# Six attention units load q in plain rows, under another instruction table, in a fused attention and bilinear-FFN kernel

## The chip, the core and the metric

The kernel runs on one core of a Trainium2 chip. A core has a matrix engine (TensorE, PE in the profile; its weight loads are PEld), a vector engine (VectorE, DVE), an activation engine (ScalarE, ACT), a general engine (GpSimd, POOL) and SyncE (SP), which here only issues DMAs. Each engine takes its instructions in program order and waits on semaphores for data of the others. The metric is the device time of one execution in microseconds (us); the time of a kernel is the median of its runs.

## The reference

```python
# attention, inside each chunk of 64 tokens: q, k, v are (8, 8, 576, 64)
scores = (1 / sqrt(64)) * q_c @ k_c^T      # 64x64 for each batch, head, chunk
attn   = softmax(scores)
out    = attn @ v_c
# FFN: x is (4608, 512); w_a, w_b (512, 1536); w_out (1536, 512)
x = out.transpose(0, 2, 1, 3).reshape(4608, 512)
y = ((x @ w_a) * (x @ w_b)) @ w_out
```

Inputs and output are float32; the kernel computes in bfloat16 with float32 sums.

## The kernel before

The 4608 tokens are nine blocks (K = 0 to 8) of 512 tokens; a block is two units of 256 tokens (units 0 to 17), and a unit is four chunks of 64 tokens with all eight heads. Blocks 0 to 3 and 5 to 8 lie in one batch entry each; block 4 (units 8 and 9) collects the ninth chunk of all eight.

**A unit of attention.** q, k and v of a unit come from HBM by DMA (`load_paired`, `load_natural`, `load_split`, all through `load`, L359) into float32 buffers `f`, of which there are two sets (even and odd units). A cast to bfloat16 (`cast_natural` for q and k into `qkb`, `cast_v` for v into `vb`, both through the helper at L330) goes to ACT, DVE or POOL as the table says. One DMA transposes q and k together (`turn_dma`, L684) into `qkT`. The scores are 32 matmuls of 64x64 (L732) into two banks; two ACT instructions take the exponential of a bank each, 128x512, and write it to `E` in bfloat16 (`part_scores`, L884). From unit 8 (`FROM`) on the values are 32 matmuls with `E` as weights and `vb` as the moving operand (L792, `part_first` and `part_second`, 16 each); DVE takes the reciprocals of the sums and multiplies (L806, L808), and a DMA transposes the block (`turn_x`, L690) into `xT`. Units 4 to 7 use another form with separate sums and values (L742, L770).

**Paired rows.** For units in `PAIRED` (4 to 17) q is loaded with two tokens side by side in a partition, so that the DMA moves runs of 512 bytes: one DMA of 512 KB for a unit within one batch entry (`load_paired`). For other units q is loaded as k is, in rows of 256 bytes, by two DMAs of 256 KB (`load_natural`). The cast of a paired q writes with a rearranged pattern, and the query order inside a chunk is then (r, q) in place of token order. For units of `PAIRED` from 8 on the exponential puts this right: it writes `E` through `p (a q r) -> p a r q`, so that consecutive elements go to every second bfloat16. Units below 8 put it right in a later DVE multiplication.

**The FFN.** Blocks 1 to 8 use a scheme with seven products in place of eight for each of the two input products (L1008, four matmuls of 128x128 by 256 columns each) and for the output product (L1313, six matmuls; L1151 for block 8). ACT and DVE copy and add the results between products (L330, L1046, L1341), and DVE or POOL make sums of inputs and of weights (L968, L1270, L1042). Block 0 uses plain products (L919).

**The order.** Everything that the kernel does is a list of operations numbered as they are made. The text `ORDER_OF_ALL` is a table of words: a letter for the engine (a: PE, b: ACT, c: DVE, d: POOL, e: SP or ACT issuing a DMA), the operation's number, and for PE the PSUM banks that it takes (of eight). Each engine runs its words in the table's order. The words were made beforehand by a planner with a cost for each operation; `c_act(n)` is the cost of an ACT instruction of n columns, 0.591 us for 512. When the kernel is built the costs are no longer used: only the table and the operations' data dependences count. A POOL operation also waits for the last bfloat16 operation of DVE ahead of it in the table.

Of the kernel before, what the change touches and what calls it, by code (L numbers as in the profile page):

```python
# [97 lines left out]
c211 d266 a344 e275 c342 b347 a349:7 b345 e44 a339:3 c215 d278 a353 e276 c340 a359:1 a350 a348:0 d268 d272 c219 b354  # L98
c355 b351 b360 c352 a372:3 c373 d356 a357:5 b358 c371 a361 c362 a365 c366 a367 c368 b47 a375 e38 a363 b376 a379:3 a377
c364 d41 d253 d45 b378 a390:4 a381 b382 c343 c383 a380:6 a384 a388:0 a401:7 b279 c249 c255 a403:2 a396 e223 b385 a394  # L100
a392 b389 a406 d242 c386 a398 b39 b391 d228 d254 c397 b407 c402 a408 c404 b393 a412 b413 a431:3 e225 b229 c399 c244
a432 a411:7 a419:2 c241 c250 c243 c252 b409 a415 b416 a420 b421 c270 e280 a317:56 a422 b319 b423 b318 e230 a434 e277
# [3 lines left out]
c418 a447:0 a534:5 a449:7 a527:4 e301 b325 c430 e304 e324 b326 e327 b448 a544 a530 b531 a525:1 d461 c450 a532 b533  # L106
c456 a536 a567:2 d469 a539 e323 e500 c526 d462 a535:6 a555:1 c528 c537 a546 a569:4 d464 d446 b306 e473 b540 c538 c541
e504 c568 b307 b547 a548 c549 b570 a556 e474 c470 c542 d471 d465 a590 a550 c551 a552 c553 e308 d335 a594:0 a592 a585:7
c586 a587:5 c588 b591 a596 a603:6 b593 b545 b597 c598 a595:7 a599 d466 e506 b600 e503 a607 b604 b608 c557 c601 a611
c612 a620:5 a609 c610 a613 c614 d529 c621 a625 b626 d472 d602 a496:12 b498 a336:04 b338 c615 a558 a559 a605:7 b337  # L110
a488:25 e475 c560 e476 b497 a514:40 b489 e459 e305 a631 a622:1 c606 c623 e477 c632 a627 c628 b516 d589 d467 b515 b517
a563 a564 b490 b491 a518:20 c520 c519 d485 d316 a492:41 a629:5 a646 c493 c633 a634 a630:0 a561:2 e499 e502 e505 d624
d554 d638 a562 e501 c494 a644:4 b565 b635 c636 a648 c468 c639 c641 b511 b647 c649 e507 a708:1 a650 c651 e460 d616 e659
a642:6 a652 c653 b645 a715 a710:7 b643 a713 a750:5 d640 c716 a722 c709 a718:0 a752:1 c654 e478 b512 a571 c714 a719
c566 e457 c711 a572 a717:7 c723 d637 c724 a574 a735 e481 e479 e510 e509 e480 b486 b720 a729 c721 b753 a733 a775 e508
a731 d581 c736 c751 b730 b776 c734 c573 a773 e513 b774 a770:0 c771 a768:6 c769 c732 a779 a680:73 a575 c576 a782 c783
a777:0 a778:6 c784 d618 d521 b681 b780 b682 a693:74 c697 c695 c698 d655 d617 d656 d737 e487 a522:23 b524 a790 a792
e484 e482 e483 d666 d657 b495 b523 b791 e685 c725 c781 c696 e458 e688 a796 c797 d619 d582 a726:3 d583 c793 a727 a794
c795 a694:47 d712 d584 d772 d658 b728 a669:25 c673 a670:61 c677 c678 c699 a741 a788:0 e686 c674 c701 c675 c700 a742
a786:1 c702 a813:5 b789 e689 e580 e579 e684 c671 c672 c676 a810 c811 a805:4 b787 a808 c809 a803:7 a744:2 e683 b690  # L120
a814 a817 c804 c806 c818 e661 e665 c819 b691 a738:6 a739 c740 a745 e703 c815 a812:7 a835 b743 a746 a747 b748 c816 a829
b830 a831 a827:4 c807 c766 c836 c749 b828 a825:6 b826 e660 e687 b667 d821 c822 c824 c764 a833 c832 c834 a754 a842:5
e692 a755 b756 a847 b848 b704 a844:1 a849 b850 c843 a757 d798 d823 a853 c837 a920:0 b854 a758 a882:73 d765 d785 c845
a851:5 c759 c855 e668 d801 d820 d840 d799 e662 e664 e578 e663 a856 b857 a852:1 a863 c858 b884 a918:2 c919 e896 e874
e900 a867 c868 b921 b864 e902 e899 a865 c866 b883 a951:3 c952 a956 a953:6 c954 a869 b957 a962 b963 c870 a958 b959
a932:57 a705:43 a933:61 b707 e577 b706 c935 c941 c936 d800 d679 c937 c942 c938 a973 b974 a965 b966 a860:5 c939 a906:31
c838 d839 d871 a907:47 c912 c914 c908 c913 c940 e873 e875 e872 e877 a961:2 c967 c915 a861 b903 b862 a960:4 a971:6 c972
c910 c911 c964 a975 a888 a889 a969:7 d841 a977 e897 c909 a979 a993 c890 e878 e945 c978 c980 c994 a986:1 a988:3 b970
d846 e762 c981 a885:4 a886 c987 d955 a991 b992 e901 e898 b880 a891:2 a892 a1000 e763 e876 c989 b1001 a997 c802 c887
d859 a893 a995:1 c976 b998 c999 a894 a1012 b1013 d879 d767 b895 e881 c947 c948 a1016 c1017 d1004 a996:3 a1027:4  # L130
a1008:0 b1009 a1010:7 a922 a923 a1025:1 d1005 c1002 c949 a1018 b904 c1007 c1006 b1011 c924 c1028 a1030 c1026 a1014
b1031 c1019 c917 e905 a1035:5 a1032 b1033 d968 d916 c1015 c990 e1081 e1079 d1020 a1036 e1058 b1037 a1034:4 c1038
a1103:1 e761 e1056 a1039 b1040 d1003 d1021 d982 a925 a1101:3 c1041 a926 c927 e760 b946 e1082 e931 a1050 c1051 a1138:6
b1104 b1102 c1139 a1046 a1048 b1047 c1049 a1052 a934:24 a1065:60 b1066 b1067 a1140:7 c1053 c1023 c1141 e1055 a1145
a1143 a1119:56 a1120:07 c1126 e1080 b944 d1042 c1127 d1142 c1124 c1128 c1125 d1022 c1129 c1122 c1123 d1054 d1024
a1043:4 b1146 a1152 b1144 a1149 b943 a1089:06 a1090:27 c1095 c1097 c1091 c1096 c1098 b1153 a1044 a1147:5 b1150 c1151
a1148:2 c1154 a1156:7 a1162 d1155 c1093 c1092 b1157 b1045 a1164 c1165 a1178 c983 c1094 a1068:0 a1166 c1167 c1029 e1057
d1087 a1173:5 c1174 b1179 a1184 b1185 c985 a1158:6 c1159 c984 c1168 a1160 a1071 b1062 e1132 d1191 d1192 b1161 c1163
a1074:2 a1075 a1199 a1175:5 c1176 d1169 e1060 e1084 b1086 b1063 a1180 a1072 b1073 a1069 a1182:3 c1070 a1183:1 b1181
c1186 a1187 b1188 a1076 a1195:5 b1196 b1200 c1189 e930 e1083 c1194 d1193 d1177 e1085 b1133 a1203 c1204 a1197:0 a1217  # L140
c1218 c1198 d950 d1190 a1205 c1206 a1222:7 a1212:3 c1213 d1134 a1201 a1077 b1078 a1219 a1214:1 c1215 c1100 a1223 c1202
b1220 b1224 a1105 a1106 a1233 b1107 a1226 b1227 a1221:3 a1108 c1135 c1170 c1225 e1061 e1059 d1099 e1267 e1088 a1252:16
b1254 c1228 a1109 c1110 a1237 a1288:4 a1235 c1238 b1234 c1236 a1239 b1289 b1253 a1326 c1240 b1327 a1302:65 c1307
a1303:23 c1311 c1309 c1305 d1136 d1207 e1064 a1121:10 e1270 e1269 c1310 e1242 e1111 e1247 e1268 c1306 a1321:7 e1113
a1332 c1322 c1308 c1312 a1290:2 c1291 a1255:6 b1130 b1131 d1210 a1276:10 a1277:75 c1284 c1280 a1323:3 c1282 c1281
c1324 c1278 b1333 a1343 b1344 a1328 a1330:0 c1334 c1279 e1272 c1283 d1216 a1339:4 a1331:3 c1340 d1208 d1229 d1209
d1137 d1211 d1172 c1285 b1329 a1335 b1274 e1117 e1248 b1336 c1337 a1347 c1348 c1325 e928 a1230:1 a1361 a1231 a1341:7
c1342 a1356:5 c1357 a1349 c1350 a1358:0 c1359 b1362 a1363 a1367 a1365:5 a1345 b1364 a1261:3 a1262 b1368 a1382 b1383
a1370 d1241 e929 e1245 e1266 e1315 a1378:0 a1366:4 c1232 e1116 a1258 d1338 d1351 c1369 b1379 c1374 c1360 c1375 a1400
a1259 c1346 c1352 d1171 d1377 b1273 b1371 c1372 a1386 c1387 b1260 b1401 a1384 c1385 c1373 c1376 a1380:2 a1388 c1389  # L150
c1381 a1404:5 a1395:7 a1263 a1256 a1406 c1396 b1407 e1246 e1243 a1397:4 b1286 e1244 e1118 e1271 e1115 c1257 e1275
d1317 d1250 c1318 a1264 b1265 a1402 b1403 c1408 b1249 c1398 a1450:7 c1287 a1420 c1421 a1416 c1417 d1390 a1479:6 d1391
d1353 c1393 c1392 a1409 a1292 a1293 b1451 b1410 a1425:45 c1480 d1316 d1354 a1405:0 c1411 a1418 c1419 e1114 e1251 c1412
a1295 a1296 c1297 a1422 c1423 d1399 a1452:6 a1484 b1427 b1426 d1355 a1464:54 c1468 b1294 a1465:12 a1304:30 c1466 c1470
b1453 a1486 b1485 a1490 e1298 b1314 a1481:0 d1424 d1394 c1469 c1472 c1471 c1467 c1473 d1319 b1313 a1440:41 a1439:35
# [20 lines left out]
def kernel(  # L176
# [159 lines left out]
    def c_act(n):  # L336
        return 0.156 + n * 0.00085
# [1360 lines left out]
```

## Time and profile before

| | |
|---|---|
| median of 3 runs | 291.56 us (291.33 to 291.64) |
| the profiled execution, its own time | 291.75 us |
| its span, first to last instruction | 290.0 us |
| ACT busy | 171.5 us (59%) x292 |
| DVE busy | 244.8 us (84%) x484 |
| POOL busy | 181.5 us (63%) x176 |
| DMA packets | 133304, 57.71 MB, mean 199 GB/s |

The span leaves out 1.75 us of the execution's own time. A busy time counts any moment at which the engine has an instruction in work, so a matrix engine that is busy nearly all the time may still lose time in short waits: these are seen in the distance between the starts of its groups of matmuls.

### The profile page before, as it was taken

To read this page: it belongs to the slowest core of one execution; us is meant where nothing else is said; L and a number is where in the kernel's file an instruction comes from. 1 tells how busy PE (TensorE), PEld (TensorE's weight loads), DVE (VectorE), ACT (ScalarE), POOL (GpSimd) and SP (SyncE) were. 2 spreads that over 40 slices of the span, in tenths; PEclk is the share of its full clock that TensorE was granted. 3 is DMA by queue.
4 is the path that set the end of the run, shared out by engine and by line. 5 is a ranking of instruction groups with operands and counts; after the bars stand their busy time and mean duration, and the time that the engine had idled before them with its cause. 6 is when DMAs were issued, how large, how long until landed. Compare 5 with 4: busy or idle time off the path is not lost.

```text
span 290.0 us, 8654 instructions
## 1 busy us (share of the span) xinstructions
PE 284.4 (98%) x3508; PEld 233.5 (81%) x3508; DVE 244.8 (84%) x484; ACT 171.5 (59%) x292; POOL 181.5 (63%) x176
## 2 busy tenths in 40 slices
PE   7999999999999999999999999999999999999995
PEld 3555458888887888888888888888888888888884
DVE  2777989999988999996897889679979787988972
ACT  3875897879658746636826674846456743245111
POOL 4626268737689688919758685689838954653130
PEclk9999999999999999999999999999999999999999
DMA  7999999879999898876997893998881540021025
GB/s 248 390 397 402 291 304 328 221 171 243 229 181 234 242 215 242 196 151 163 259 247 190 213 288 85 222 205 240 193 200 41 178 111 0 2 110 38 0 107 186
DMA packets 133304, 57.71 MB, mean 199 GB/s; under 512 B 103952, under 2 KB 124560, under 8 KB 133264
## 3 DMA queue, kind: packets, MB, share of 16 engines
q1 hardware_dynamic: 132032, 56.05, 72.0%
q10 hardware_dynamic: 1232, 1.11, 1.1%
q8 instruction: 27, 0.44, 0.6%
q14 instruction: 13, 0.11, 0.1%
HBM read 37.75 MB, written 9.44 MB: 163 GB/s over the span
## 4 chain that ended last, share of the span: by engine, by line
PE 91%; DVE 4%; DMA 1%; ACT 1%; issue 1%; POOL 0%; DVEq 0%; ACTq 0%
PE F L1008 49%; PE F L1313 23%; PE F L919 7%; PE F L1151 3%; PE F L528 2%; PE F L732 1%; PE F L1642 1%; PE F L792 1%; DMA f<-in_k_dram 1%; ACT E L884 1%; DVE wst L1255 1%; DVE bsb L1046 1%; DVE AB L1046 1%; DVE AB L1042 0%; DVE osb L1341 0%
## 5 line engine op out<-in xcount | busy, mean ns | idle before, releaser
L330 ACT COPY part<-F 128x512 f32<-128x512 f32 x94 | 54.2, 590 | 57.1 <-PE F L1008 37.4
L1042 POOL TENSOR_TENSOR AB<-AB,bsb 128x512 bf16<-128x512 bf16 x43 | 49.5, 1157 | 27.7 <-DVE AB L1042 9.4
L1046 DVE TENSOR_TENSOR bsb<-F,part 128x512 bf16<-128x512 f32 x72 | 49.0, 684 | 6.3 <-PE F L1008 4.8
L1270 POOL TENSOR_TENSOR wst<-AB 128x512 bf16<-128x512 bf16 x31 | 35.6, 1155 | 12.9 <-DVE wst L968 4.3
L1008 PEld LDWEIGHTS <-WA 128*128 128x128 bf16 x384 | 37.2, 98 | 5.1 <-issue 0.3
L1008 PEld LDWEIGHTS <-WB 128*128 128x128 bf16 x384 | 37.2, 98 | 4.7 <-issue 0.3
L330 ACT COPY wst<-F 128x512 f32<-128x512 f32 (+1 forms) x42 | 23.4, 570 | 29.4 <-PE F L1313 12.2
L1046 DVE TENSOR_TENSOR AB<-F,part 128x512 bf16<-128x512 f32 x48 | 32.9, 685 | 6.5 <-PE F L1008 3.1
L1313 PEld LDWEIGHTS <-AB 128*128 128x128 bf16 x288 | 28.0, 98 | 3.5 <-issue 0.2
L1008 PEld LDWEIGHTS <-Ta 128*128 128x128 bf16 x288 | 28.0, 98 | 3.4
L1008 PEld LDWEIGHTS <-Tb 128*128 128x128 bf16 x288 | 27.7, 98 | 3.7 <-issue 0.2
L1313 PEld LDWEIGHTS <-wst 128*128 128x128 bf16 x288 | 28.0, 98 | 3.3
L1008 PE MATMUL F<-wst,WB 128*128 128x256 bf16 x192 | 28.8, 273 | 0.1
L1008 PE MATMUL F<-wst,Ta 128*128 128x256 bf16 x192 | 28.8, 273 | 0.0
L1008 PE MATMUL F<-wst,Tb 128*128 128x256 bf16 x192 | 28.8, 273 | 0.0
L1008 PE MATMUL F<-xT,WA 128*128 128x256 bf16 x192 | 28.7, 273 | 0.0
L1008 PE MATMUL F<-wst,WA 128*128 128x256 bf16 x192 | 28.7, 273 | 0.0
L1008 PE MATMUL F<-xT,WB 128*128 128x256 bf16 x192 | 28.3, 273 | 0.0
L330 ACT CAST qkb<-f 128x1024 bf16<-128x1024 f32 (+1 forms) x25 | 24.3, 983 | 3.7 <-DMA f<-in_k_dram 3.7
L1313 PE MATMUL F<-WO,AB 128*128 128x256 bf16 x192 | 25.2, 273 | 0.2 <-ACT E L884 0.2
L884 ACT ACTIVATE E<-F 128x512 bf16<-128x512 f32 x32 | 21.1, 699 | 5.3 <-PE F L732 5.2
L1270 POOL TENSOR_TENSOR spare_sum<-AB,wst 128x512 bf16<-128x512 bf16 x17 | 19.6, 1154 | 6.7 <-DVE WB L956 3.5
(137 smaller groups left out, 542.4 us busy)
## 6 DMA issues: line engine op xcount, KB each, us to landing
f<-in_k_dram SPq DMA_DIRECT2D x28, 256.0 KB, 4.8
out_dram<-osb SPq DMA_DIRECT2D x28, 256.0 KB, 2.9
f<-in_q_dram SPq DMA_DIRECT2D x12, 512.0 KB, 5.6
f<-in_v_dram SPq DMA_DIRECT2D x40, 128.0 KB, 3.5
f<-in_v_dram SPq DMA_DIRECT2D x16, 256.0 KB, 5.3
wst<-in_moe_w_b_dram SPq DMA_DIRECT2D x6, 512.0 KB, 8.6
wst<-in_moe_w_a_dram SPq DMA_DIRECT2D x6, 512.0 KB, 8.9
wst<-in_moe_w_out_dram SPq DMA_DIRECT2D x6, 512.0 KB, 4.4
```

The source lines that it names most:

```text
L330: return A.copy(out=out, in_=in_) if e == "act" else ENG[e].tensor_copy(out=out, in_=in_)
L528: T.transpose(turned()[:, r, :], qkb[hu][:, x, mm * 512 + r * 128:mm * 512 + r * 128 + 128], identity)
L732: T.matmul(score_at(u, PS[j][cl * 64:cl * 64 + 64, c:c + 64]), chunk_of(u, 1, m, j, chunk_at(u, g, cl)), chunk_of(u, 0, m, j, chunk_at(u, ...
L792: T.matmul(f_of(PA[cl])[c * 64:c * 64 + 64, n * 65:n * 65 + 65], E[u % 2][cl * 64:cl * 64 + 64, j, m * 128 + g * 64:m * 128 + g * 64 + 64] ...
L884: op("act", c_act(512), lambda e, at=at: A.activation(out=at()[0], in_=at()[1], func=AF.Exp, scale=scale), r=[("ps", id(PS[j]))], w=[("E", ...
L919: T.matmul(f_of(b)[:, 0:n].rearrange("p (u t) -> p u t", u=len(us)), w[ft][:, kt, :], x[:, us[0]:us[-1] + 1, kt, :], start=(kt == 0), stop ...
L1008: T.matmul(f_of(bank)[:, q * 256:q * 256 + 256], lhs(2 * g + q, kt), rhs[:, kt, :], start=(first and q == 0 and kt == 0), stop=(q == 1 and ...
L1042: op(("dve", "pool"), TIMES, lambda e: ENG[e].tensor_tensor(out=dst, in0=dst, in1=b, op=MULT), r=bk, w=key, prio=-300, fast=True)
L1046: op("dve", c_dve(512), lambda e: V.tensor_tensor(out=dst, in0=two(f_of(bank)), in1=two(pab[s][i]), op=ADD), r=[("ps", id(bank)), ("part", ...
L1151: T.matmul(f_of(bank)[:, 0:256], lhs[:, i, h], rhs[:, i, :], start=(first and i == 0), stop=(i == NP - 1), skip_group_check=True)
L1270: op(*long_op(hs), lambda e, i=i, x=x, y=y, o_=o_: ENG[e].tensor_tensor(out=SS[i][:, s], in0=x[:, s], in1=y[:, s], op=o_), r=fts + [(name, ...
L1313: T.matmul(f_of(bank)[:, at:at + 256], lhs[:, i, tt * 128:tt * 128 + 128], rhs[:, i, :], start=(first and at == 0 and i == 0), stop=(i == ...
```

## The change

Three edits. `PAIRED` ends at unit 11, so q of units 12 to 17 is loaded by `load_natural` (two DMAs a unit, 256-byte rows), cast without rearranging, and its exponentials read and write contiguously. The cost given to an exponential that writes with the stride is 0.17 us longer (an argument of the planner, unused when the kernel is built). And the table is another one from its 296th word on. The six added loads move the numbers: an operation that had number n has n + 1 above 872, and n + 2 to n + 6 after each further unit, n + 6 in the end.

```diff
-    PAIRED = range(4,18)
+    PAIRED = range(4,12)
...
-                op("act", c_act(512), lambda e, at=at: A.activation(out=at()[0], in_=at()[1], func=AF.Exp, scale=scale),
+                op("act", c_act(512) + (0.17 if u in PAIRED and u >= FROM else 0), lambda e, at=at: A.activation(out=at()[0], in_=at()[1], func=AF.Exp, scale=scale),
...
-c211 d266 a344 e275 c342 b347 a349:7 b345 e44 a339:3 c215 d278 a353 e276 c340 a359:1 a350 a348:0 d268 d272 c219 b354
...
-d256 c395 c433 c245 a410:1 a435 b436 e321 a424 c251 c414 c417 d248 c247 a328:63 b329 d374 c425 a290:05 b291 b330 e226
-b289 a426 a439 a440 b441 b292 c246 c405 c369 c387 a437:6 a428 a438 c427 d400 e227 d288 e320 b331 a309:04 a332:35 c442
-c333 c334 b311 e322 d463 a451 a452 b310 b312 c429 a313:14 d443 c315 c314 c444 e302 e303 a454 a543:3 a455 c445 c453
...
-b1104 b1102 c1139 a1046 a1048 b1047 c1049 a1052 a934:24 a1065:60 b1066 b1067 a1140:7 c1053 c1023 c1141 e1055 a1145
-a1143 a1119:56 a1120:07 c1126 e1080 b944 d1042 c1127 d1142 c1124 c1128 c1125 d1022 c1129 c1122 c1123 d1054 d1024
...
-a1295 a1296 c1297 a1422 c1423 d1399 a1452:6 a1484 b1427 b1426 d1355 a1464:54 c1468 b1294 a1465:12 a1304:30 c1466 c1470
-b1453 a1486 b1485 a1490 e1298 b1314 a1481:0 d1424 d1394 c1469 c1472 c1471 c1467 c1473 d1319 b1313 a1440:41 a1439:35
...
-c1712 b1713 a1715 e1714 c1719 e1720 c1716 e1717
+c211 d266 a344 e275 c342 b347 a349:7 b345 e44 a339:3 c215 d278 a353 e276 d270 c340 e38 d268 c219 a350 a348:1 b354 c355
...
+c387 c433 e277 a437:2 a424 a439 a440 b291 c425 b441 d289 a438 e227 a309:74 b331 b311 a332:16 c252 e226 c288 a313:35
+a451 a452 c374 c430 c442 b310 b312 a454 d400 d467 e321 c333 c334 c469 c315 c314 e320 b325 e322 b326 d443 c444 c453
...
+c1004 a1016 b881 a1014 b1015 c1017 a887 c888 a1020 a997:4 e876 a894 a895 c1021 b918 b896 e897 d906 d841 c950 e947
+a1010:1 a1012:6 c1006 a1036:5 c1001 d1007 d1009 c919 e898 a1018 b905 e902 e904 a1027:2 c1019 a1029:3 b1011 a1032 c1028
...
+a936:15 b946 b1070 c1143 e903 d948 e1084 e761 a1054 c1055 a1050 c1051 a1153 a1107:7 c1023 b1069 a1123:50 c1128
...
+c1472 c1474 b1459 a1310:64 b1319 d1430 d1325 d1326 a1471:17 a1496 b1497 c1475 c1476 c1478 c1477 c1473 c1479 a1492
+d1360 b1320 a1487:3 c1488 a1507 a1445:61 a1446:04 a1419:7 a1420 c1451 c1452 c1453 c1454 c1447 c1449 c1450 d1489 d1418
...
+a1717 c1718 b1719 e1720 d1618 d1653 a1724 c1725 e1726 a1721 c1722 e1723
```

The words that matter below. Unit 4: loads of v 226 and 227, cast of v 288 (d: POOL before, c: DVE after), values 313, and the two output products 451 and 452, which stand ahead of 313 before and behind it after; 321 and 322 load k of unit 7, and 321 stands ahead of 226 before and behind it after. Unit 13: scores 1065 (1068 after), exponentials 1066 and 1067 (1069, 1070), first values 1119 (1123). Unit 16: scores 1304 (1310), first values 1440 (1445). Unit 13's q in two loads 897 and 898, with the transposing DMA 947 of block 5 between them. The number of operations on each engine, before and after: PE 580 and 580, ACT words 296 and 298, DVE 481 and 487, POOL 168 and 160, DMAs on SP 201 and 207. Among the moved ones two of the six casts of the output weights (words 41 and 45) go from POOL to ACT, and twelve more of the 512-wide sums of L1270 go to DVE than leave it. The first 77 PE words are the same in both tables.

More of the change, by code (lines that the diff above doesn't have):

```diff
@@ new lines @@
+a1186:5 c1183 e1085 b1091 a1188 c1172 c1178 d1103 e1059 a1191 b1192 d1066 d1181 a1071:0 a1072 c1076 a1079 a1187:2
+c1189 a1203 c1190 a1080 a1205 c1073 c1193 a1209 c1194 a1207 b1204 e1136 c1195 c1206 a1201:4 b1202 a1199:6 a1218:0
+d1196 b1200 e1086 e1057 c1210 e1087 a1216:1 c1065 a1294:7 a1223 a1221 e1272 a1077:2 a1078 d1137 d1197 b1081 c1217
+c1219 a1226:1 c1208 e1092 c1224 b1222 a1227 c1228 a1225:0 c1229 c1104 a1230 b1231 d1138 d1198 a1327:5 a1109 b1295
+c1175 a1237 a1110 b1111 c1139 c1232 c1238 a1241 a1112 e1067 c1328 d1173 a1113 a1243 c1114 c1244 a1296:3 b1297 e1246
@@ new lines @@
+b1368 b1370 a1373 a1376 c1377 a1351 b1374 c1375 a1388 c1352 a1372:6 c1378 e1253 e1117 e1274 a1390 b1254 b1389 e1120
+a1386:4 d1140 d1366 a1392 c1393 a1234:0 e1116 a1384:3 b1385 a1235 b1236 e1251 d1214 d1380 a1394 c1381 a1406 c1383
+c1323 c1382 a1263 b1407 c1357 c1395 a1401:5 c1402 b1387 a1403:6 c1404 c1262 a1264 a1410:5 a1412 d1280 d1358 b1265
+a1268 a1408 a1485:6 b1413 a1269 a1422 c1396 c1414 c1379 c1391 a1456:2 e1249 c1457 b1255 b1409 b1270 e1119 c1293 a1298
+d1359 d1324 a1415 a1411:1 d1397 d1398 c1486 d1405 a1426 c1427 d1399 e1277 b1322 e1250 b1423 b1416 a1299 b1300 a1490
@@ new lines @@
+a1530:3 a1522:6 a1546 b1547 c1523 e1305 e1480 d1538 a1542:0 a1534 a1440:6 c1533 d1539 d1524 b1439 b1535 c1536 a1550
+a1544:4 a1548 c1551 c1545 b1543 a1552 a1435 a1442 c1553 a1443 a1561:5 a1441 c1549 c1554 c1537 a1564 d1540 c1436 b1444
+a1566 c1562 a1460 b1565 a1570 b1567 e1307 d1481 a1601:3 a1559:2 a1568:1 a1573 e1306 c1455 c1516 c1517 c1541 c1483
+c1560 c1518 c1482 b1571 c1555 a1461 c1574 a1463 d1556 c1572 a1580 a1569:5 a1603:2 b1602 d1557 c1581 d1563 a1584 c1462
+c1575 c1585 a1624 b1625 a1464 c1558 e1467 a1637:0 a1586 a1621:7 a1619:1 b1604 a1626 a1582 c1576 c1465 e1466 e1468
@@ new lines @@
+e1469 c1587 b1627 a1630 c1620 b1631 c1583 c1622 d1519 a1628:6 a1633 d1588 d1484 c1632 a1654:5 a1629:1 a1639:4 a1656:7
+b1634 d1623 b1638 a1659 a1641 c1635 b1640 c1657 d1636 a1661 a1645 a1647 c1655 c1646 c1648 c1662 d1649 b1642 b1660
+a1595:7 a1685:3 a1596 a1643 c1615 c1644 a1668 b1669 a1665 a1687:5 a1664:6 c1650 b1666 c1670 a1663:1 a1672 b1673 c1667
+d1671 a1577:2 a1678 a1578 b1579 a1676 c1677 c1679 a1686 a1674 c1675 c1658 a1592 a1593 c1594 a1689:0 c1680 c1616
+a1589:1 a1590 a1690 a1597 a1691:6 a1598 a1692 c1591 c1651 c1652 b1599 c1617 c1600 a1688 a1697 a1700 a1693 b1694 c1681
@@ L172 @@
+c1701 c1682 a1605 a1695 c1696 c1698 e1699 a1608 a1609 c1610 a1606 e1702 e1613 c1684 a1703 b1607 e1611 c1683 c1704
+a1706 a1708:4 e1612 e1614 b1707 a1713 b1714 a1709 a1727 a1705:1 c1728 c1715 e1729 e1716 b1710 c1711 e1712 b1730 b1731
+a1717 c1718 b1719 e1720 d1618 d1653 a1724 c1725 e1726 a1721 c1722 e1723
 """
```

108 lines of the change are left out of this document (43 added, 65 removed).

## The prediction

> **What bounds the kernel now.** I read the page first, for the engines, then the waits of the matrix engine (columns: us in total, times, longest).
>
> ```profile
> span 290.0 us, 8654 instructions
> PE 284.4 (98%) x3508; PEld 233.5 (81%) x3508; DVE 244.8 (84%) x484; ACT 171.5 (59%) x292; POOL 181.5 (63%) x176
> ...
> PE F L1313 <- ACT E L884: 0.2, 1, 0.2
> ```
>
> TensorE sets the end. Its work is the same in both tables (580 operations, the same matmuls), so the change can gain only what TensorE still loses, and lose as much as new waits make. After its start-up there is one wait long enough for the list, 0.2 us for an exponential. Shorter losses are seen in the timeline of TensorE (start, duration, group): a product of 4 matmuls of 256 columns takes 0.44 us to the next start, six take 0.66, twelve 1.31.
>
> ```profile
> 68.97 1.48 PE L1313 MATMUL F<-wst,AB 128*128 128x256 bf16 x12
> 70.54 0.45 PE L770 MATMUL F<-E,vb 64*64 64x64 bf16 x32
> ...
> 170.46 0.52 PE L792 MATMUL F<-vb,E 64*64 64x65 bf16 x32
> 171.16 0.38 PE L1313 MATMUL F<-WO,AB 128*128 128x256 bf16 x2 [0.17 <-ACT E L884]
> ...
> 197.47 0.60 PE L1008 MATMUL F<-wst,Tb 128*128 128x256 bf16 x4
> 198.09 0.39 PE L792 MATMUL F<-vb,E 64*64 64x65 bf16 x24
> ...
> 229.37 0.60 PE L1008 MATMUL F<-wst,Tb 128*128 128x256 bf16 x4
> 229.97 0.60 PE L1008 MATMUL F<-xT,WA 128*128 128x256 bf16 x4
> 230.56 0.45 PE L792 MATMUL F<-vb,E 64*64 64x65 bf16 x32
> ...
> 260.25 1.47 PE L1313 MATMUL F<-WO,AB 128*128 128x256 bf16 x12
> 261.83 0.38 PE L1008 MATMUL F<-wst,WB 128*128 128x256 bf16 x2
> ```
>
> A change from products to attention costs 0.09 us on entry and 0.10 on return, which the next rows show (the chain of waits: start, length, piece): the group behind an attention visit takes 0.76 in place of 0.66, and a first group of scores 0.37 in place of 0.29.
>
> ```profile
> 194.10 0.66 PE F L1313 x6
> 194.75 0.37 PE F L732 x32
> 195.13 0.76 PE F L1313 x6
> ...
> 198.55 0.29 PE F L732 x32
> ```
>
> Less that, the losses are: at 170.46 to 171.16, 0.70 for 32 matmuls of values, which take 0.38 elsewhere (two groups of 16 and the return), so 0.32; at 229.37, 0.60 - 0.44 = 0.16, and 0.59 - 0.44 - 0.09 = 0.06 behind it; at 197.47, 0.62 - 0.44 - 0.09 = 0.09. These 0.63 us stand in front of or behind values that wait for exponentials (at 229.97 a product takes the bank that an exponential of unit 16 frees). The others that I looked up: 1.57 - 1.31 - 0.09 = 0.17 at 68.97 and 1.58 - 1.31 = 0.27 at 260.25, together 0.44 us.
>
> **The change part by part.** *The exponentials.* The view of L884 in two windows, up to 110 us (units 2 to 7, contiguous) and after (units 8 to 17, strided):
>
> ```profile
> L884 ACT ACTIVATE E<-F x12: 592/605/632, 25.9 to 90.5; 128x512 bf16<-128x512 f32 x12
> ...
> L884 ACT ACTIVATE E<-F x20: 727/751/819, 111.3 to 229.8; 128x512 bf16<-128x512 f32 x20
> ...
>   PEld L792: 1.2, 5
> ```
>
> Same shape, 751 against 605 ns. Twelve of the twenty become contiguous: 12 x 0.146 = 1.75 us off ACT, which is 59% busy, so that is worth nothing by itself. What counts is the path from scores to values, where two or three exponentials run one after the other. In the old table three products of four (1140, 1145, 1143: 1.31 us) cover the exponentials of unit 13, and three those of unit 16; two strided ones alone take 1.50. In the new table it is four (1054, 1050, 1153, 1107: 1.75 us) beside the scores of unit 12, and four for unit 16 (1496, 1492, 1487, 1507), and two exponentials take 1.21. So the 0.63 us go. Bounds: 0.2 (the one listed wait) and 1.2 (the weight loads' whole wait for `E`, of which the pipeline hides a part); I take 0.63, worked out on TensorE itself.
>
> [...]
>
> *Visits.* Counting runs of attention words among the PE words behind the common part, I find 22 in the old table and 21 in the new. One visit fewer: 0.09 + 0.10 = 0.19 us less (between 0 and that).
>
> *q in plain rows.* Each of six units issues one DMA more on SP, and 1024 packets of 512 bytes become 2048 of 256: 6144 more packets.
>
> ```profile
> q1 hardware_dynamic: 132032, 56.05, 72.0%
> ...
> 130.00:205.00 75.00, 74.81 (x1022) 65.38 (x1020) 62.72 (x139) 47.43 (x78) 57.23 (x52) 1.00 0.86 211
> ...
> L359 SPq DMA_DIRECT2D f<-in_q_dram x6: 426/635/682, 135.7 to 201.6; - x6
> ...
> f<-in_k_dram SPq DMA_DIRECT2D x28, 256.0 KB, 4.8
> f<-in_q_dram SPq DMA_DIRECT2D x12, 512.0 KB, 5.6
> ```
>
> SP: 6 x 0.635 = 3.8 us more of issuing over the 75 us from 130 to 205; SP then stands still before most transposes. Transfers: nothing if bytes decide; if packets do, 72% of 16 x 290 us over 132032 packets is 25 ns a packet, and 6144 of them over 16 engines are 9.7 us, against (1 - 0.86) x 75 = 10.5 us that are free. I take no loss: the trace's average packet is already near 256 bytes (k and v have such rows), so the true price lies between, and q is loaded ahead. The tightest case is unit 13: load 898 stands behind the transposing DMA 947 in SP's queue. In order behind it come a landing (4.8), a cast (1.05, row below) and a transpose (3.9), about 10 us; between the words 898 and 1068 stand 16 products, 8 us, but SP reaches the words earlier than TensorE reaches their neighbours. If that cover were gone TensorE would stand up to 2 us.
>
> ```profile
> L330 ACT CAST qkb<-f x9: 1048/1055/1104, 130.2 to 213.3; 128x1024 bf16<-128x1024 f32 x9
> ```
>
> These nine are q and k mixed, with and without a rearranged write, and within 5%: the plain cast gains nothing.
>
> *The rest of the table.* The other 0.44 us are dealt anew, and I have no reason for less or more. One thing speaks for more: a bank or a sum that DVE has to return. From the last start of a product to the next start on its result go 0.16 us (a matmul lasts 273 ns and the next starts after 109), 0.09, 0.69 and 0.05:
>
> ```profile
> L1008 PE MATMUL F<-wst,WB 128*128 128x256 bf16 x192 | 28.8, 273 | 0.1
> ...
> 256.50 0.03 issue
> 256.52 0.02 DVEq L1046
> 256.55 0.04 issue
> 256.59 0.69 DVE bsb L1046
> ...
> 261.78 0.04 issue
> ```
>
> That is 0.99 us. Behind the common part the old table leaves no such return under 0.98 us of TensorE's work, the new one three of 0.85. Each is worth 0 to 0.14; as two follow each other and can share a wait, I take 0.15 in all, of 0 to 0.42.
>
> **Sum.** -0.63 - 0.19 + 0.15 = -0.67 us. The profiled execution's 291.75 (span 290.0 and 1.75 around it) would become 291.1; it lies 0.19 above the median of the runs, and from the median, 291.56, I get 290.9. The last matmuls, the last additions and the last store are in the same order in both tables, so nothing is taken there.
>
> **The rivals.** *No change (291.5).* The waits for exponentials go, but as many others come: the sum would be -0.19 + 0.15. For it: 0.44 us of losses without any exponential show that a table leaves such. To the same time leads that the edit does not do what it says: stride and time of day go together in the rows, so the 146 ns could come from what else runs after 110 us; then two exponentials keep 1.5 us, though the wider cover holds even then.
>
> *Slower (292.7): unit 4's v.* Before, it is cast on POOL at 69.45 and its values start at 70.54, 0.17 late.
>
> ```profile
> 62.23 2.23 SPq L359 DMA_DIRECT2D f<-in_v_dram  x2
> ...
> 69.45 1.03 POOL L330 CAST vb<-f 128x1024 bf16<-128x1024 f32 x1
> ...
> L330 DVE CAST vb<-f 128x1024 bf16<-128x1024 f32 x1 | 0.7, 683 | 0.0
> ...
> f<-in_v_dram SPq DMA_DIRECT2D x16, 256.0 KB, 5.3
> L330 ACT CAST WO<-wst 128x1024 bf16<-128x1024 f32 x4 | 4.3, 1078 | 0.0
> ```
>
> The new table has values 313 ahead of products 451 and 452, 1.31 us earlier: 70.37 - 1.31 = 69.06. The cast goes to DVE (0.68), so v must have landed by 68.3. The second load, issued near 63.4, lands near 68.7; load 321, which stood ahead of it, now stands behind, 0.62 less, 68.1. That fits by 0.2 us. But two casts of output weights (2 x 1.08) move to ACT, ahead of unit 5's and unit 4's k casts, behind which SP's transposes and then these loads wait. If ACT's idle time does not take them up, v lands 2.2 us later, TensorE stands 2.0 us, and DVE, which waits at the head of its queue, holds back the additions behind it: 290.9 + 2.0 - 0.2 = 292.7. Against it: ACT waits 37.4 us in all for products of L1008, some of it there. It decides from a landing later than about 68.3.
>
> ```profile
> L330 ACT COPY part<-F 128x512 f32<-128x512 f32 x94 | 54.2, 590 | 57.1 <-PE F L1008 37.4 <-DVE bsb L1046 11.6 <-DVE inv L808 4.3
> ```
>
> *Slower by transfers (293).* If packets decide, DMA has 0.8 us left in 75 and each late load of units 12 to 17 costs up to the 2 us above; one such is 292.9. [...]
>
> **How the numbers follow.** Forecast 0.49, no change 0.18, unit 4 0.23, transfers 0.10. A measurement of this kernel tells about 0.2% from no change: 290.98 to 292.14. So faster 0.49, same 0.18, slower 0.33. The forecast's own range goes from 290.1 (exponentials at 1.2) to 291.3 (0.2 for them); the whole one to 292.9, where the transfers would end.
>
> **What would show it.** Right: the exponentials after 150 us at 0.60 to 0.63; weight loads of L792 waiting under 0.5 us for `E`; six q loads of 512 KB where there were twelve, and twelve of 256 KB; no loss at the values of units 13 and 16. Wrong: twelve exponentials still near 0.75; a gap of TensorE near 69 released by a DVE cast; waits of PE for `qkT`; other gaps that sum to over 1.3 us after 45 us.

## The result, and the profile after

The changed kernel takes 290.08 us (median of 21 runs, 289.76 to 291.67), the kernel before 291.72 beside it (21 runs): a ratio of 0.9938, 95% interval 0.9923 to 0.9952. That is 1.64 us less, on the side that was forecast, but two and a half times the 0.67 us of the sum and 0.02 us below the stated range.

The profiled execution took 289.98 us. The page's first lines and its queue of loads, then the waits of the matrix engine (us in total, times, longest), then the exponentials behind 150 us (min/median/max in ns, and who waited for them), and those between 110 and 150 us, seven of the eight of units 8 to 11:

```profile
span 288.2 us, 8683 instructions
PE 282.2 (98%) x3508; PEld 232.6 (81%) x3508; DVE 245.3 (85%) x490; ACT 170.7 (59%) x294; POOL 172.5 (60%) x168
...
q1 hardware_dynamic: 138272, 56.05, 73.9%
```

```profile
PE F L1642 <- DVE zero L1418: 1.3, 1, 1.3
PE F L528 <- POOL qkb L330: 0.5, 1, 0.5
PE F L528 <- ACT qkb L330: 0.4, 1, 0.4
```

```profile
L884 ACT ACTIVATE E<-F x12: 591/597/652, 167.7 to 229.0; 128x512 bf16<-128x512 f32 x12
...
  PEld L792: 0.2, 1
```

```profile
L884 ACT ACTIVATE E<-F x7: 727/754/767, 109.4 to 141.6; 128x512 bf16<-128x512 f32 x7
```

TensorE still sets the end. The wait for an exponential is off the list, the twelve exponentials take 597 ns where those still strided take 754, and the weight loads of the values wait 0.2 us for `E` where they waited 1.2. No wait for `qkT` is there, so the loads of q are in time.

To see where the time went I cut the span at two places that both kernels have. The first is the last product of the part in which the tables are word for word the same, the second the last addition of DVE. The timeline of TensorE has the one and the chain of waits the other; before:

```profile
45.66 0.60 PE L1008 MATMUL F<-wst,Ta 128*128 128x256 bf16 x4
```

```profile
286.48 0.42 DVE osb L1179
```

and after:

```profile
45.49 0.60 PE L1008 MATMUL F<-wst,Ta 128*128 128x256 bf16 x4
```

```profile
284.89 0.42 DVE osb L1179
```

Up to the first cut 0.17 us are gone, between the cuts (from here on "the middle") 240.82 - 239.40 = 1.42, and behind the second (290.0 - 286.48) - (288.2 - 284.89) = 0.21: together the 1.8 us of the spans. The first piece is chance: in eleven other profiles of kernels that are the same up to there, this product stands between 45.33 and 45.90. The other two are not, as the experiments show.

In the middle I took each group's distance to the next start, less what its matmuls and a change of work cost, as in the prediction. Waits of 0.04 us and more, in us:

```
before                                              after
70.5   0.16  POOL's cast of unit 4's v              59.7   0.28  ACT copy, held by a DVE addition
98.1   0.10  DVE multiplication of unit 6           69.4   0.05
106.8  0.16  DVE addition
117.4  0.21  DVE addition (L1075)
170.7  0.07  \
171.2  0.24   |
198.1  0.09   |  exponentials (0.67)
230.0  0.16   |
230.6  0.06   |
231.0  0.05  /  (an ACT copy behind them)
261.8  0.27  DVE addition
```

Some of these are in the prediction's rows; the three others of before are these (start, duration, group): nine matmuls at 97.00 take 1.08 to the next start in place of 0.98, six at 105.97 take 0.81 in place of 0.66, and 117.66 is 0.74 behind 48 matmuls of values that take 0.53.

```profile
97.00 1.15 PE L1313 MATMUL F<-WO,wst 128*128 128x256 bf16 x9
98.08 0.49 PE L1008 MATMUL F<-xT,WA 128*128 128x256 bf16 x3
...
105.97 0.82 PE L1313 MATMUL F<-WO,spare_sum 128*128 128x256 bf16 x6
106.78 0.49 PE L1008 MATMUL F<-wst,WA 128*128 128x256 bf16 x3
...
116.92 0.80 PE L792 MATMUL F<-vb,E 64*64 64x65 bf16 x48
117.66 0.61 PE L1313 MATMUL F<-TS,wst 128*128 128x256 bf16 x4
```

The last of them stands inside the 48 values: one of their matmuls starts 0.19 us behind the one ahead of it, at 117.40, as soon as this addition of DVE, which reads a bank, has ended (117.35):

```profile
116.66 0.69 DVE L1075 TENSOR_TENSOR AB<-F,bsb 128x512 bf16<-128x512 f32 x1
```

So the exponentials gave 0.67 us and the waits for other engines 0.89 - 0.33 = 0.56. What is left of the 1.42, 0.19 us, is the size of the one attention visit that went: the matrix engine goes from products to attention 22 times in the middle of the trace of before and 21 times in that of after.

### The profile page after: what moved, and what is told of

It reads as the page before. It is cut to its first block, busy times and chain, and to the rows that moved or that the text cites. A ratio compares the mean times of both kernels' runs of the same rounds, so it can differ in the third digit from the quotient of the medians.

```text
span 288.2 us, 8683 instructions
## 1 busy us (share of the span) xinstructions
PE 282.2 (98%) x3508; PEld 232.6 (81%) x3508; DVE 245.3 (85%) x490; ACT 170.7 (59%) x294; POOL 172.5 (60%) x168
## 3 DMA queue, kind: packets, MB, share of 16 engines
q1 hardware_dynamic: 138272, 56.05, 73.9%
## 4 chain that ended last, share of the span: by engine, by line
PE 92%; DMA 4%; DVE 1%; POOL 1%; ACT 0%; issue 0%; SPq 0%; ACTq 0%
PE F L1008 51%; PE F L1313 25%; PE F L919 7%; PE F L1151 3%; DMA wst<-in_moe_w_b_dram 2%; PE F L732 2%; DMA f<-in_q_dram 1%; PE F L792 1%; PE F L742 1%; PE F L528 1%; PE F L770 0%; POOL WB L330 0%; PE F L1642 0%; PE F L757 0%; DVE bsb L330 0%
## 5 line engine op out<-in xcount | busy, mean ns | idle before, releaser
L330 ACT COPY part<-F 128x512 f32<-128x512 f32 x97 | 55.9, 591 | 50.7 <-PE F L1008 28.6
L1042 POOL TENSOR_TENSOR AB<-AB,bsb 128x512 bf16<-128x512 bf16 x47 | 53.7, 1155 | 16.9 <-DVE AB L1042 5.1
L1270 POOL TENSOR_TENSOR wst<-AB 128x512 bf16<-128x512 bf16 x25 | 28.7, 1154 | 5.1 <-DVE wst L1270 1.9
L330 POOL CAST qkb<-f 128x512 bf16<-128x512 f32 (+1 forms) x20 | 15.9, 805 | 23.1 <-DVE wst L968 8.3
L1008 PE MATMUL F<-wst,Ta 128*128 128x256 bf16 x192 | 28.8, 273 | 0.1
L1008 PE MATMUL F<-wst,Tb 128*128 128x256 bf16 x192 | 28.8, 273 | 0.0
L330 ACT CAST bsb<-F 128x512 bf16<-128x512 f32 x30 | 17.8, 599 | 11.7 <-PE F L1008 8.7
L330 ACT CAST qkb<-f 128x1024 bf16<-128x1024 f32 (+1 forms) x21 | 20.1, 968 | 2.8 <-DMA f<-in_k_dram 2.8
```

What stands on the lines that cost most here:

```text
L330: return A.copy(out=out, in_=in_) if e == "act" else ENG[e].tensor_copy(out=out, in_=in_)
L1008: T.matmul(f_of(bank)[:, q * 256:q * 256 + 256], lhs(2 * g + q, kt), rhs[:, kt, :], start=(first and q == 0 and kt == 0), stop=(q == 1 and ...
L1042: op(("dve", "pool"), TIMES, lambda e: ENG[e].tensor_tensor(out=dst, in0=dst, in1=b, op=MULT), r=bk, w=key, prio=-300, fast=True)
L1270: op(*long_op(hs), lambda e, i=i, x=x, y=y, o_=o_: ENG[e].tensor_tensor(out=SS[i][:, s], in0=x[:, s], in1=y[:, s], op=o_), r=fts + [(name, ...
```

## The experiments

Two theories at first. A: the new table carries the gain itself. B: the short exponentials carry it. C is the price of the 256-byte rows. All ratios are to the kernel before on the same chip, since that differs by 0.3 us from one to another (291.72 to 291.99).

**Order and layout apart.** In `order_alone` the second halves of the q loads are taken out of the new table and the numbers set back; in `layout_alone` they are put into the old one, each behind its first half.

```diff
 order_alone, against the changed kernel
-    PAIRED = range(4,12)
+    PAIRED = range(4,18)
 layout_alone, against the kernel before
-    PAIRED = range(4,18)
+    PAIRED = range(4,12)
 new_strided, against the changed kernel
-                    if u in PAIRED and u >= FROM:
+                    if u >= FROM:
 old_contig, against the kernel before
-                    if u in PAIRED and u >= FROM:
+                    if FROM <= u < 12:
```

> The new table with q of units 12 to 17 still paired: the second halves of the q loads left out of it, the one load of 512 KB at the place of the first half, the exponentials of units 8 to 17 strided (0.75 us). Theory A (the table itself carries the gain: it takes away the waits for DVE, POOL and a cast, 0.56 us, one attention visit, 0.19 us, and covers two exponentials with four products, 1.75 us, which holds for 2 x 0.75 us too): 290.1 to 290.4 us, no wait of TensorE for an exponential over 0.1 us. Theory B (the short exponentials carry it: with strided ones this table waits at the values of units 13, 15, 16 and 17 as the old one did, 0.6 us in all): 290.6 to 290.9 us.

> The old table with q of units 12 to 17 in plain rows: the second q load directly behind the first, the exponentials of units 12 to 17 contiguous. Theory A: the waits for exponentials at 170.5 to 171.2, 197.5 and 229.4 to 231.0 go (0.6 of their 0.67 us), the other 0.9 us of waits stay: 290.9 to 291.2 us. Theory B: most of the 1.6 us comes with the edit alone, 290.1 to 290.5 us. Theory C (256-byte packets cost TensorE time, and the new table only hides that by earlier loads): 291.6 us or more.

> The changed kernel with the strided write kept in the exponentials of units 12 to 17; q is loaded in plain rows all the same, so the output of these units has its queries in another order. Against the changed kernel only 12 exponentials are longer (0.75 in place of 0.60 us). Theory A: 290.0 to 290.3 us, the wider cover takes them. Theory B: 290.6 to 290.9 us.

> The kernel of before with the exponentials of units 12 to 17 written contiguously, q still loaded paired, so the output of these units has its queries in another order. Theory A: 290.9 to 291.2 us, as with plain q under the old table, because the loads cost nothing. Theory C: 0.3 us or more below plain q under the old table, the difference being the price of the 256-byte packets.

In the table, short and strided say how the exponentials of units 12 to 17 write; q of these units is in plain rows in `layout_alone`, `new_strided` and the changed kernel.

```
                                  us      ratio (95%)              middle  last store lands after
before                            291.7   1                        240.82  2.06 us
old_contig    old table, short    291.30  0.9983 (0.9975, 0.9992)  240.17  2.22
layout_alone  old table, short    290.88  0.9970 (0.9961, 0.9979)  240.28  1.71
order_alone   new table, strided  290.56  0.9959 (0.9947, 0.9971)  239.91  1.68
new_strided   new table, strided  290.69  0.9964 (0.9952, 0.9976)  240.14  1.70
changed       new table, short    290.08  0.9938 (0.9923, 0.9952)  239.40  1.71
```

Read by the middle, the two causes add up. The whole edit, short exponentials and plain q, is worth 0.54 us under the old table (240.82 to 240.28) and 0.51 under the new one (239.91 to 239.40); the table is worth 0.91 without the edit (240.82 to 239.91) and 0.88 with it (240.28 to 239.40). Short exponentials with the loads left as they are give 0.65 under the old table (240.82 to 240.17) and 0.74 under the new one (240.14 to 239.40). Of the 0.74, 0.22 are not theirs: two pauses of TensorE in `new_strided`, 0.08 at 95.1 and 0.14 at 167.6, inside groups of attention, where it waits for no semaphore, and which neither `order_alone` nor the changed kernel has. So of the 1.42 the table has about 0.9 and the exponentials about 0.5: A and B each hold in part. In `layout_alone` the waits for exponentials are gone just where they were (timeline of TensorE): the values at 170.31 follow their product after 0.53 us, 0.44 and the 0.09 of the entry, and take 0.38.

```profile
169.78 0.60 PE L1008 MATMUL F<-wst,Tb 128*128 128x256 bf16 x4
170.31 0.45 PE L792 MATMUL F<-vb,E 64*64 64x65 bf16 x32
170.69 0.83 PE L1313 MATMUL F<-WO,AB 128*128 128x256 bf16 x6
```

The half of A that fell is its cover of four products. In the timelines of ACT, then TensorE, of `order_alone`, three exponentials, one of unit 12 and the two of unit 13, stand between the scores and the values of unit 13, not two:

```profile
167.93 1.94 ACT L884 ACTIVATE E<-F 128x512 bf16<-128x512 f32 x3 [0.26 <-PE F L732]
```

```profile
169.92 0.46 PE L792 MATMUL F<-vb,E 64*64 64x65 bf16 x32 [0.23 <-ACT E L884]
```

and in the changed kernel:

```profile
167.66 1.57 ACT L884 ACTIVATE E<-F 128x512 bf16<-128x512 f32 x3 [0.26 <-PE F L732]
```

```profile
169.35 0.45 PE L792 MATMUL F<-vb,E 64*64 64x65 bf16 x32
```

The strided three end at 169.87 and the values start 0.05 behind them; the short three end at 169.23, 0.12 before TensorE comes. The new table has room for three short exponentials there, with 0.12 us to spare, and not for three strided ones.

C is not seen. `layout_alone` is 0.11 us above `old_contig` in the middle, and that is the wait for unit 4's v at 70 us (0.27 against 0.15), ahead of every load that the edit touches. The price is there, but free: in the trace of before, packets of 256 bytes take 18.9 ns on the mean, those of 512 bytes 28.8, so six units cost (12288 x 18.9 - 6144 x 28.8) / 16 = 3.5 us more on each DMA engine.

**The end.** The last store, 128 KB, lands 2.06 us after its issue in `before` and 2.22 in `old_contig`, but 1.7 in the four others. The DMA view of the last microseconds shows what differs (of a queue: packets, MB, share; of an issue: KB each, median us to landing): before (286.2 to 289.2 us)

```profile
q1 hardware_dynamic: 460, 0.41, 39.0%
q14 instruction: 1, 0.01, 1.5%
...
out_dram<-f SPq DMA_DIRECT2D x1, 128.0 KB
out_dram<-osb SPq DMA_DIRECT2D x1, 128.0 KB, 2.1
```

and after (284.6 to 287.6):

```profile
q1 hardware_dynamic: 512, 0.46, 43.9%
...
out_dram<-f SPq DMA_DIRECT2D x1, 128.0 KB, 1.7
out_dram<-osb SPq DMA_DIRECT2D x1, 128.0 KB, 1.7
```

A packet of the instruction queue, 8 KB of code, goes at 286.80 and takes 0.72 us; the last eight packets of 1 KB of the store then come one by one, 0.04 us apart, where each takes 0.044 to 0.046, as from one DMA engine that is late; which engine moves them is not shown. In `old_contig` the code goes at 286.30, in `layout_alone` at 289.55, behind the last store, in the changed kernel at 277.06. Whose code is it?

```diff
 old_memsets
+idle = buf("idle", [128, 8], BF16)        (behind zero, ahead of the load buffers)
             made = o["fn"](o["eng"])
+            if o.get("n") == 125:
+                for i in range(20):
+                    V.memset(idle, 0.0)
 old_act
             made = o["fn"](o["eng"])
+            if o.get("n") in (1500, 1520, 1433, 1529, 1541, 1539, 1438, 1559, 1565, 1596, 1456, 1598):
+                A.copy(out=zero[:, 0:1], in_=zero[:, 1:2])
```

> The kernel of before with 20 tiny memsets more on DVE, right behind its first instruction, where it idles for 4 us. If the 8 KB of instructions that the instruction queue moves at 286.8 us, while the last stores are written, are DVE's, they are moved some 10 us earlier: the last store then lands 1.7 us after its issue in place of 2.06, and the time is 291.2 to 291.5 us, 0.25 to 0.5 us below before. If the fetch is another engine's, or the late store is chance, 291.65 to 291.8 us, with the fetch still behind 286 us.

> The kernel of before with 12 tiny copies of one column on ACT, one behind each of 12 ACT instructions between 236 and 255 us, on a tile that is dead by then; no buffer moves. The 20 memsets on DVE did not move the 8 KB of instructions away from the last stores, so they are not DVE's; the instructions that the trace counts on ACT at that moment are nearly the same in all kernels (446 to 448), so I take them for ACT's. If so, they are moved 10 us earlier or more, the last store lands 1.7 us after its issue, and the time is 0.25 to 0.45 us below before. If not, the fetch stays behind 286 us and the time is that of before, or up to 0.2 us more for the copies.

The 20 instructions more on DVE left the code where it was, 3.1 us before the end; that kernel took 297.62 us (ratio 1.0185, 1.0156 to 1.0213), for another reason that is found below. The 12 on ACT moved it to 268.12. The last store then lands after 1.68 us, the middle stays (240.79), and the time is 291.19 us, ratio 0.9974 (0.9952 to 0.9996), the kernel before without a change to its order. So I take the code for ACT's. A count bears this out: in the traces of the six kernels in the table, of these two and of three more, ACT has run 446 to 448 instructions, waits and issues included, when the code goes, whether that is at 268 or at 289 us. The new table gives ACT 461 of them in place of 450, so it comes to the 446th some 10 us earlier. That the new table's end is shorter for this reason rests on the count; it was not tried on the new table itself.

**Are the waits separate?** Theory D says so: each is worth its length. E: the order counts as a whole. `old_mended` takes the five waits of the old table that have nothing to do with exponentials out of `layout_alone`, `after_fix` the largest of the new one.

```diff
 old_mended, against layout_alone (words of its table)
-d400 e227 d288
+e227 d288 d400
-c633 ... c494
+c494 c633 ...
-a735 ... a729
+... a729 a735
-d619 d582
+d582 d619
-a1645 a1637:0
+a1637:0 a1645
 after_fix, against the changed kernel
-c395 d228 b39 c248 c241 d254 c399
+c395 d228 b39 c248 d254 c399 c241
 after_fix2, against the changed kernel
+c395 d228 b39 c399 c248 c241 d254
 all_plain, against the changed kernel (and two second halves in the table)
-    PAIRED = range(4,12)
+    PAIRED = range(4,8)
```

> The old table with plain q (layout_alone, 290.88 us), and five words moved, one for each wait of TensorE in it that has nothing to do with an exponential: POOL's cast of unit 4's v ahead of a product of POOL (the wait at 70.4, 0.16 to 0.27 us), DVE's last multiplication of unit 6 ahead of an addition (97.9, 0.10), the product on a DVE addition behind the product that follows it (106.6, 0.155), POOL's output sum of block 2 ahead of another (117.5, 0.217), and a product on a DVE addition behind the one that follows it (261.0, 0.264). Theory D (the two tables differ by separate waits, each at one place, that are paid back one for one): 0.8 to 1.0 us less, 289.9 to 290.1 us, the time of the changed kernel without a word of its table. Theory E (the gain belongs to the order as a whole; a wait that is taken away comes back elsewhere): 0.4 us less or not even that, 290.5 us or more.

> The changed kernel with one word moved: DVE's sum of output weights (243's first step, 241) from ahead of the addition 399 to behind it, so that the copy 409, which overwrites what that addition reads, is done 0.5 us earlier. The largest wait of TensorE in the changed kernel, 0.28 us at 59.7, hangs on that copy. Theory D: 0.2 to 0.28 us less than the changed kernel, 289.8 to 289.9 us, the first version below both. Theory E: no change, 290.0 to 290.1 us.

> The changed kernel with q of units 8 to 11 in plain rows too, and so eight exponentials more written contiguously, 8 x 0.15 us less of ACT. In the changed kernel TensorE waits for none of these exponentials by more than 0.03 us. Theory D (a shorter exponential is worth what TensorE waits for it, nothing else): 289.95 to 290.15 us, no change. Rival (each strided exponential costs in proportion, 0.6 us for twelve): 0.4 us less, 289.7 us. If the 256-byte rows have a price it shows as a longer time, 290.3 us or more.

`old_mended` took 290.56 us, ratio 0.9951 (0.9940 to 0.9963), middle 240.00: 0.28 us less than `layout_alone`, not 0.8 to 1.0. Four of the five waits, 0.79 us, are gone. That at 117.6 (0.19) stayed, because the word that was moved, a sum of POOL, was not its cause: TensorE stands there until the DVE addition of L1075 ends, at 117.57, as it did before. New waits came at 73.4 (0.10), 102.6 (0.06) and 109.2 (0.23), 0.39 in all, and besides them a pause of 0.17 at 95.0 at no semaphore, of the kind seen in `new_strided`. The last wait is seen in DVE's timeline, first of `layout_alone`, then of `old_mended`:

```profile
107.26 0.69 DVE L1046 TENSOR_TENSOR AB<-F,wst 128x512 bf16<-128x512 f32 x1
107.87 0.68 DVE L330 COPY part<-F 128x512 f32<-128x512 f32 x1
```

```profile
106.80 0.68 DVE L1046 TENSOR_TENSOR bsb<-F,part 128x512 bf16<-128x512 f32 x1
107.86 0.69 DVE L1046 TENSOR_TENSOR AB<-F,wst 128x512 bf16<-128x512 f32 x1 [0.38 <-PE F L1008]
108.46 0.68 DVE L330 COPY part<-F 128x512 f32<-128x512 f32 x1
```

The product that was moved back by one feeds an addition, DVE waits 0.38 us for it at the head of its queue, and the copy behind it is what the product at 109.20 needs. The time is as E had it; but half of the 0.79 stayed gone, so a wait is neither all its own nor all the order's.

`after_fix` took 290.32 us, ratio 0.9944 (0.9932 to 0.9956), middle 239.70: the wait at 59.7 went, and one of 0.58 came at 63.1. There DVE's sum 241 now ran beside POOL's sum 254 and took 1.32 us in place of 0.69. So the mending itself could be at fault, and a second one kept the two apart.

> The changed kernel with the addition 399 moved ahead of the two output weight sums 248 and 241, which POOL's sum 254 still follows, so that no bf16 sum of DVE runs beside it. Theory D (a wait is worth its own length where the mending delays nothing else): TensorE's wait at 59.7 (0.28 us) goes, none comes, 0.2 to 0.28 us less than the changed kernel, 0.9930 of before. Theory E (it comes back elsewhere): 0.9937 or more, with another wait of 0.1 us or more.

290.29 us, ratio 0.9949 (0.9937 to 0.9962), middle 285.12 - 45.41 = 239.71. The wait went again (59.38, the six matmuls take 0.65) and one of 0.52 came 3 us later:

```profile
58.73 0.82 PE L1313 MATMUL F<-WO,AB 128*128 128x256 bf16 x6
59.38 0.60 PE L1008 MATMUL F<-wst,Ta 128*128 128x256 bf16 x4
...
61.39 0.82 PE L1313 MATMUL F<-WO,AB 128*128 128x256 bf16 x6
62.57 0.60 PE L1008 MATMUL F<-wst,WA 128*128 128x256 bf16 x4 [0.36 <-DVE AB L1046]
```

The timelines of POOL and DVE say why; first the changed kernel, then this one:

```profile
58.50 1.15 POOL L1270 TENSOR_TENSOR wst<-wst,AB 128x512 bf16<-128x512 bf16 x1 [1.11 <-DVE wst L1255]
```

```profile
58.93 0.68 DVE L1046 TENSOR_TENSOR AB<-F,part 128x512 bf16<-128x512 f32 x1
59.53 0.68 DVE L1270 TENSOR_TENSOR wst<-wst,AB 128x1024 bf16<-128x1024 bf16 x1
```

```profile
59.01 1.15 POOL L1270 TENSOR_TENSOR wst<-wst,AB 128x512 bf16<-128x512 bf16 x1 [1.71 <-DVE wst L1255]
```

```profile
58.85 0.69 DVE L1046 TENSOR_TENSOR AB<-F,part 128x512 bf16<-128x512 f32 x1
59.45 1.27 DVE L1270 TENSOR_TENSOR wst<-wst,AB 128x1024 bf16<-128x1024 bf16 x1
```

In the changed kernel two additions that read a bank (`F`; 0.69 us from 58.33 and 0.68 from 58.93) run beside POOL's 1.15 us, and the sum of two SBUF operands starts 0.12 us before POOL ends (59.53 against 59.65) and takes 0.68. With one addition moved ahead, POOL starts half a microsecond later, and the sum runs into it: 1.27 us. POOL ends at 60.16 there, and 0.56 us behind that the sum is done. What the two contend for, no run shows. The sums of 512 columns in the changed kernel behave alike. Alone they take 0.42; three that start with 0.24, 0.65 and 0.99 us of a POOL sum still to run (at 207.51, 232.71 and 148.24) take 0.52, 0.94 and 1.27, the rest of POOL's sum and 0.28 more.

`all_plain` took 290.26 us, 0.9945 (0.9930 to 0.9960), middle 239.61. Eight exponentials less with a stride bring nothing, as D said: TensorE did not wait for them. Its middle is 0.21 us above the changed kernel's for a wait of 0.24 at 50.4, behind a cast of output weights, long before the first load that differs. By the whole time `after_fix`, `after_fix2` and `all_plain` are not told from the changed kernel (0.9938, 0.9923 to 0.9952); what is said of them rests on the middle of one profile each.

**Which waits are the table's.** The changed kernel once more.

> The changed kernel once more, for which waits and which tail belong to the table and which to one execution. If the accounting of the waits is right, the same four groups stand late (59.7, 69.4, 112.1, 227.8), with 0.28 us at the first, and none of the five waits of the old table shows; the first 45 us differ by up to 0.3 us, as they do between kernels that are the same there. Time 0.55 to 0.7% below before.

290.28 us, ratio 0.9939 (0.9917 to 0.9960), middle 239.41 against 239.40, the same late groups at 59.7 (0.28), 69.3 (0.05), 112.0 (0.03) and 227.8 (0.04) and no other. `old_act`, which has the old table, has all eleven of the old waits again, none off by more than 0.03 us. A late load can upset this. `old_tile_last` (below) has the old table too, and its profiled execution took 292.46 us, 0.97 more than its median:

```profile
95.55 0.45 PE L770 MATMUL F<-E,vb 64*64 64x64 bf16 x32 [0.72 <-POOL vb L330]
```

POOL's cast of a v waited 1.01 us for the load there, TensorE lost 0.91 us in front of these values, and the waits of 0.10 at 98.1 and 0.27 at 261.8 are missing, as they would be if the late engines had caught up by then; that was not looked into.

**The place of the buffers.** In `old_memsets`, 5.6 us above its runs of before, the queue of the loads is busy for 81.5% of the span in place of 72.0%, with the same packets. Its tile of 16 bytes moves all the load buffers, and the other buffers behind them. Three kernels of before with such a tile, one memset and nothing else:

```diff
 old_shift16 (64 bytes: [128, 32])
+idle = buf("idle", [128, 8], BF16)        (ahead of the load buffers)
 old_tile_last
+idle = buf("idle", [128, 8], BF16)        (behind all other buffers)
```

> The kernel of before with one unused tile of 16 bytes a partition ahead of the load buffers (one memset writes it), as in the kernel with the 20 memsets. If the 5.6 us there come from the place of the buffers (all of them 16 bytes further), the time is 4 to 7 us above before and 256-byte packets take 22 to 24 ns on the mean in place of 18.9. If they come from the memsets, the time is that of before within 0.3 us.

> The same with 64 bytes. If a buffer that starts at an odd multiple of 16 bytes is what costs, 64 bytes cost nothing: the time of before within 0.3 us, 256-byte packets at 19 ns. If any other place costs, 4 us or more above before.

> The kernel of before with the same unused tile of 16 bytes a partition, made behind all other buffers, so that none of these moves. If their place costs the 5 us, the time is that of before within 0.3 us and 256-byte packets take 19 ns on the mean. If the tile or its memset costs it, 4 us or more above before.

298.01 us (ratio 1.0224, 1.0186 to 1.0261), 297.12 (1.0178, 1.0142 to 1.0214) and 291.49 (0.9993, 0.9983 to 1.0002). It is the place: 256-byte packets take 23.0 and 22.5 ns on the mean in the first two, 19.3 in the last. `old_shift16`, the queue's line and that of k's loads, which land after 4.8 us before:

```profile
q1 hardware_dynamic: 132032, 56.05, 82.7%
...
f<-in_k_dram SPq DMA_DIRECT2D x28, 256.0 KB, 5.7
```

That an odd multiple of 16 bytes is what costs is refuted by the 64; what about the place it is stays open.

## Why the prediction was off

**TensorE sets the end, and only its waits count**: right. Every change of the time is one of its starts or of the last store.

**The exponentials, -0.63**: right in size, 0.5 to 0.65 by the runs, 0.67 by the waits that went. Wrong was the cover: the prediction counted two exponentials under the four products in front of unit 13's values, there are three. Three short ones still fit, by 0.12 us that the prediction did not know of, which is luck; and its remark under "no change" that the cover holds with strided ones too falls with the wait of 0.30 us in front of the values at 169.92 of `order_alone`. The strided form costs time: 754 ns against 597 contiguous in the same kernel. It also splits its pattern into runs of 32 on the side that it reads; whether that or the strided write is what costs was not tried. `new_strided` settles the rival that the 146 ns came from the time of day: it differs from the changed kernel only in how the twelve are written, and they take 749 ns there in place of 597.

**One visit fewer, -0.19**: the visit went, 22 to 21, and its price fits by what is left over; it was not tried alone.

**q in plain rows, 0**: right. 3.5 us of DMA, between the 0 and 9.7 that bounded it, and hidden; no wait for `qkT`. The rival by packets had a true premise, that a byte costs more in a small packet (those of before took 74 ps for a byte at 256 bytes, 56 at 512 and 43 at 2048), and no way to the time. The mean packet of before is not near 256 bytes, as the prediction has it: 56.05 MB in 132032 packets are 425 bytes, though 100352 of them have 256.

**"The other 0.44 us are dealt anew, and I have no reason for less or more", then +0.15 for short returns of DVE**: this is the step that failed. The three short returns cost nothing: behind the common part no wait over 0.04 us is left but the one at 59.7, for an ACT copy, and the one at 69.4. The waits for DVE, POOL and the v cast, 0.89 us in all (the 0.44 of the prediction and three that it had not looked up), went, and 0.33 came. The mistake was to take such waits for a rate, so many per table, when a second profile of the same table, but for the late load of `old_tile_last`, repeats each of them to 0.03 us. They were there to be read one by one: for each, whether the new words still have the late instruction ahead of the product. Only unit 4's cast was read so, and as a danger.

**"Nothing is taken there" (the end)**: wrong by 0.21 in the profile. The order of the work was the same; the code of ACT was not at the same place.

With these two steps the sum is -0.67 exponentials, -0.19 visit, -0.56 other waits, -0.21 end: -1.63, against 1.64 measured. That is no test of the terms, since the visit was taken as what the others left of the middle. The range was too narrow for the same reason: its lower end held the exponentials' bound and the visit (291.56 - 1.2 - 0.19 is 290.17, put down as 290.1), and nothing for the other waits.

**Unit 4's v** was cast on DVE, as foreseen, at 67.86 us, early enough for the values at 68.68: nothing stands in front of them, and the group behind them is 0.05 us late at 69.4.

## What to carry to other kernels

Where one engine is 98% busy, list every wait of it in the old trace with what ended it, and check each against the new order; do not price the lot as a mean. A wait taken away need not be worth its length: here, of 0.79 us of waits that moved words took away, 0.39 came back as other waits, and where DVE ran without a pause (57 to 64 us) the moved word made a loss of 0.3 us. Before a word is moved, the end of the wait has to be matched with the end of the instruction that is blamed for it: one of the five words here was moved for a wait that another engine's addition ended. Two instruction orders made by a planner differ by its whole layout, so judge the edit and the order by kernels that have one without the other.

## What the hardware showed besides

Code is loaded while the kernel runs: 8 KB, ACT's by the runs, that go during the last stores cost 0.4 us (last store 2.06 us against 1.68), and a dozen instructions of ACT more, between 236 and 255 us, took that cost away. It goes when ACT has run its 446th to 448th instruction, in all eleven traces counted.

A tile of 16 or 64 bytes a partition ahead of the load buffers cost 5 to 6 us of 292, through packets of 256 bytes that take 22.5 to 23.0 in place of 18.9 ns on the mean.

A DVE sum of two SBUF operands, 1024 columns, took 0.68 us alone and 1.27 to 1.32 beside a POOL sum; additions of 512 columns with one operand in a bank took 0.66 to 0.69 in the changed kernel, beside a POOL sum too. A sum of two SBUF operands of 512 columns took 0.42 alone, and three that started with 0.24, 0.65 and 0.99 us of a POOL sum still to run took that rest and 0.28 us.
